# A weight's sign carried through the shift, and a new order of work in steps 0 to 31

## The chip, the cores and the metric

The kernel runs on one core of a Trainium2 chip. A core has a matrix engine (TensorE, PE in the profile, with its weight loads listed apart as PEld), three engines for element-wise work (VectorE or DVE, ScalarE or ACT, GpSimd or POOL) and an engine, SyncE (SP), that here only issues transfers. Each engine works through its own queue in order. Matrices are multiplied from SBUF into PSUM, the memory that sums matmuls; DVE and ACT read and write both, POOL only SBUF. The metric is the device time of one execution in microseconds (us). A difference of about 0.3% is the least that can be told from none.

## The reference

```python
# retention over 8 heads, batch 8, 576 positions, head size 64
scores = scale * np.matmul(q, k.transpose(0, 1, 3, 2))
gamma = 1.0 - 2.0 ** (-5.0 - np.arange(H, dtype=np.float32))
Dmat = np.where(rel >= 0, gamma[:, None, None] ** rel[None, :, :], 0.0)
x = np.matmul(scores * Dmat[None], v)          # then as 4608 x 512
# feed-forward
h = x @ w_in                                   # 512 x 2048, float64
P = a[0] + a[1] * h + a[2] * h**2 + a[3] * h**3
Q = 1.0 + np.abs(b[0]) * np.abs(h) + np.abs(b[1]) * h**2
return ((P / (Q + 1e-06)) @ w_out).astype(np.float32)   # w_out 2048 x 512, float64
```

The two weight matrices are float64 (a float32 array times a float64 scalar), so the kernel gets them as 64-bit words and makes float32 of them itself.

## The kernel before

**Tiling.** The 4608 tokens are 36 units of 128. Retention goes unit by unit, with a running state; a *visit(a, k)* on PE finishes the outputs of unit a and makes scores and state sums of unit k. The feed-forward takes blocks of 512 tokens (four units) and 16 slices f of 128 hidden channels; one (block, slice) is a *step*. Each float32 operand is split in a high and a low part, and a product takes three matmuls, so *gemm1* of a step (x by w_in) is 12 matmuls 128x512 into a PSUM tile `h`, and *gemm2* (the step's result by w_out) 12 more into `acc`, three or four steps later. Between them DVE and ACT make P and Q of 128x512 elements: `ffn_p` (ACT makes p = a3·h + a2 and u = |h|, DVE multiplies p by h), `ffn_p2` (DVE, the last reader of `h`), `ffn_va` and `ffn_v` (ACT, DVE: the denominator), `ffn_r` (ACT: logarithm and exponential, for 1/Q), `ffn_q`, `ffn_q3` (DVE), `ffn_hi` (ACT) and `ffn_lo` (POOL up to step 23, DVE later): the two parts for gemm2. A number in brackets is the step or unit: p2(3) is `ffn_p2` of step 3.

**Two buffers for h.** The pool `ps_h` (line 95) has two tiles. They go in turn to the `h` of each gemm1 and, in a visit with both units, to a tile `y` for unit k. So gemm1 of the step after a visit waits until `ffn_p2` of the step of that visit has read its `h`, and the visit's `y` waits for `ffn_p2` of the step before it.

**Weights.** There are 32 pieces of 128x512 words: (0, f) of w_in, (1, f) of w_out. Each is loaded by SP (line 142) and taken apart by `split_weight` (line 144): ACT writes to a tile `c` the absolute value of the high word, scaled by 2^-112 as if it were a float32 (which turns the exponent field of float64 into that of float32, moved right by three bits), and leaves in place of the low word its top three bits; DVE shifts `c` left by three and puts these in; DVE then puts in the sign; ACT makes the high part of `w`, POOL the low part. These are stages: `start` runs the first, and a call of `splitN` advances each weight that stands at stage N. `split0` does nothing but advance; `split1` is the shift, `split2` the sign, `split3` the last two operations. `STARTS_BEFORE` and `STARTS` (lines 46, 48) set how many weights start when: six before step 0, then 1, 1, 2, 1, 2 and one a step to step 23. So a weight's pace follows from the place of the four `split` names in the list of a step.

**Order.** Nothing is reordered: `InOrder` (line 58) keeps the program's order on each engine, and each step calls the functions in the order of a list of names (`run`, line 513). Before step 0 units 0 to 4 are begun with `BEFORE` and `LAST_BEFORE`. Then steps 0, 2, 4, 6 and 23, which have a visit ("whole" steps), use `FIRST`; steps 1, 3, 5, 7, 21 and 22 `FIRST_ALONE`; steps 8 to 20 `MID` (where u lies in PSUM, in `free_at`); steps 24 to 31 `DENSE` (with a visit) and `DENSE_ALONE`; later ones `REST`, at the end `END`. Steps 0 to 7 are the first half of block 0, steps 8 to 23 block 1, steps 24 to 31 the other half of block 0. All engine instructions pass through one helper and stand on line 67 of the profile; groups are told apart by tile names.

Of the kernel before, what the change touches and what calls it, by code (L numbers as in the profile page):

```python
# [12 lines left out]
F32 = mybir.dt.float32  # L13
# [4 lines left out]
AF = mybir.ActivationFunctionType  # L18
ALU = mybir.AluOpType
# [12 lines left out]

BEFORE = "split1 start scale_q scale_v visit_a decay visit_b add fade keep_hi keep_lo split2 split3 split0".split()
LAST_BEFORE = "visit_b keep_hi visit_a keep_lo start split1 decay add fade scale_q scale_v split2 split3 split0".split()
FIRST = "split1 gemm1 visit ffn_p ffn_p2 ffn_hi split2 decay keep_hi ffn_lo gemm2 ffn_r scale_v scale_q split3 decay1 add fade start split0 keep_lo ffn_q ffn_q3 ffn_va ffn_v".split()
FIRST_ALONE = "split1 split3 gemm1 visit gemm2 ffn_p split2 ffn_va ffn_p2 ffn_hi decay keep_hi ffn_lo ffn_r scale_q decay1 add keep_lo fade start scale_v split0 ffn_q ffn_q3 ffn_v".split()
MID = "start split2 gemm1 ffn_p gemm2 ffn_r ffn_hi ffn_lo ffn_va split3 ffn_p2 ffn_q ffn_v ffn_q3 split0 split1".split()
DENSE = "gemm1 ffn_p visit decay split0 ffn_p2 split1 scale_q ffn_hi ffn_r ffn_va ffn_lo scale_v gemm2 ffn_q split2 ffn_v keep_hi split3 ffn_q3 keep_lo decay1 add fade".split()
DENSE_ALONE = "gemm1 ffn_p visit decay keep_hi decay1 add ffn_r split1 fade keep_lo split2 ffn_p2 split0 ffn_va ffn_v scale_q ffn_hi ffn_lo gemm2 split3 scale_v ffn_q ffn_q3".split()
REST = (  # L40
    "gemm1 ffn_p visit ffn_p2 ffn_hi decay keep_hi ffn_lo decay1 add fade keep_lo scale_q scale_v ffn_va ffn_v gemm2 ffn_r"
    " ffn_q ffn_q3"
# [28 lines left out]
def retention_ffn(ctx: ExitStack, tc: tile.TileContext, qkv, w_in, w_out, ab, masks, gq, gv, out):  # L71
# [26 lines left out]
    pe, act, dve, pool = (InOrder(tc, e) for e in (nc.tensor, nc.scalar, nc.vector, nc.gpsimd))  # L98
# [45 lines left out]
    def split_weight(k):  # L144


        nm = f"{k[0]}_{k[1]}"
        words = bits[k].bitcast(I32).rearrange("p (c w) -> p c w", w=2)
        low, high = words[:, :, 0], words[:, :, 1]
        c = cnv.tile([P, DM], I32, tag="c", name=f"c{nm}")  # L150
        cf = c.bitcast(F32)


        act.activation(cf, high.bitcast(F32), AF.Abs, scale=math.ldexp(1.0, -112))
        act.activation(low, low.bitcast(U32), AF.Copy, scale=math.ldexp(7.49, -32))
        yield
        yield
        dve.scalar_tensor_tensor(c, c, 3, low, ALU.logical_shift_left, ALU.bitwise_or)
        yield
        dve.scalar_tensor_tensor(c, high, -0x80000000, c, ALU.bitwise_and, ALU.bitwise_or)  # L160
        yield
        w = wts.tile([P, 2, DM], F32R, tag=f"w{nm}", name=f"w{nm}")
        del bits[k]
        act.activation(w[:, 0, :], cf, AF.Copy)
        pool.tensor_tensor(w[:, 1, :], cf, w[:, 0, :].bitcast(F32), ALU.subtract)
        parts[k] = w
# [331 lines left out]
    def load_weights(n):  # L498
        for k in [k for _, k in zip(range(n), loads)]:
            load_weight(k)  # L500

    def split_start(n):
        for k in [k for _, k in zip(range(n), splits)]:
            going.append([split_weight(k), 0])
            next(going[-1][0])
# [7 lines left out]
    def run(names, todo):  # L513
        todo |= {f"split{j}": (split_step, j) for j in range(4)}
        for name in names:
            if name in todo:
                todo[name][0](*todo[name][1:])
# [50 lines left out]
    for i in range(len(steps) + lag(len(steps))):  # L568
# [23 lines left out]
        whole = i in VISITS  # L592
        early = FIRST if whole else FIRST_ALONE
        dense = DENSE if whole else DENSE_ALONE
        run(END if not this else MID if free_at else early if i < first else dense if i < 2 * NF else REST, todo)
        load_weights(2)
# [41 lines left out]
```

## Time and profile before

| | |
|---|---|
| median of 3 runs | 917.73 us (916.36 to 919.26) |
| profiled execution, its own time | 915.75 us |
| its span, first to last instruction | 913.9 us |
| mean granted clock of TensorE | 0.983 |
| ACT busy | 696.2 us (76%) |
| POOL busy | 154.3 us (17%) |
| weight pieces split | 32, first ACT operation at 13.2 us, last at 188.2 us |
| gemm1 of step 0 starts | 33.09 us |

A row of a timeline gives the start in us, the duration in us, the engine, the line, the operation, the tiles as written<-read, shapes and count, and in brackets how long the engine had been idle and what released it. A row of windows gives the stretch, its length, and for each engine its busy time with the count of instructions, then the granted clock, the DMA share and GB/s. A row of groups gives the count, then the busy time in us and the mean of one in ns, then idle time before them with its releasers. On PE the rows of matmuls overlap a little, since they are pipelined.

### The profile page before, as it was taken

Reading aid. Unit: us, or ns where it says so; the run is one execution under the profiler, and the core shown is the slowest. Engines: PE = TensorE matmul, PEld = TensorE weight load, DVE = VectorE, ACT = ScalarE, POOL = GpSimd, SP = SyncE. Lnnn points to the kernel's source line nnn. Section 1 sums busy time; section 2 is a strip of 40 time slices with the busy share of each in tenths; the row PEclk is TensorE's granted clock in tenths of the full one; section 3 lists DMA queues with packets and bytes.
Section 4 is the critical chain, followed back from the end, with each engine's and each line's share of the span. In section 5 each row is a group of like instructions: output and inputs, shape, how many; then the busy total and the mean of one; then the engine's idle time right before and its main releaser. Section 6 shows DMA issues by size and latency. Waiting matters only on the chain.

```text
span 913.9 us, 19359 instructions
## 1 busy us (share of the span) xinstructions
PE 888.9 (97%) x7852; PEld 733.1 (80%) x7852; DVE 801.1 (88%) x1217; ACT 696.2 (76%) x1306; POOL 154.3 (17%) x128
## 2 busy tenths in 40 slices
PE   7888999999999999999999999999999999999997
PEld 6666778878888888888888888888888888888886
DVE  3699999998899988889888889889888998888895
ACT  5798899988667778777877787777877777667774
POOL 3556445551011110011100100010110111000000
PEclk8789999999999999999999999999999999999999
DMA  9985000014121112111211112011211121001001
GB/s 340 363 309 202 1 0 1 1 49 138 47 93 48 47 47 93 47 47 47 93 48 48 47 65 74 25 43 33 90 47 48 47 94 47 1 2 46 1 1 46
DMA packets 20569, 65.50 MB, mean 72 GB/s; under 512 B 2432, under 2 KB 2432, under 8 KB 20480
## 3 DMA queue, kind: packets, MB, share of 16 engines
q1 hardware_dynamic: 20480, 64.28, 20.0%
q8 instruction: 61, 1.00, 0.5%
q14 instruction: 28, 0.23, 0.1%
HBM read 54.83 MB, written 9.44 MB: 70 GB/s over the span
## 4 chain that ended last, share of the span: by engine, by line
PE 81%; DVE 13%; issue 2%; ACT 2%; DMA 1%; SPq 0%; ACTq 0%; DVEq 0%
PE acc L67 37%; PE h L67 35%; DVE p L67 6%; PE ps L67 4%; DVE v L67 3%; DVE c L67 3%; PE y L67 2%; PE psNone L67 2%; PE unread L67 1%; DMA gv_sb<-in_gv 1%; ACT free_at L67 1%; DMA bits<-in_w_out 0%; ACT v L67 0%; DVE qk L67 0%; ACT o L67 0%
## 5 line engine op out<-in xcount | busy, mean ns | idle before, releaser
L67 PE MATMUL acc<-w,g 128*128 128x512 f32 x1632 | 396.3, 392 | 0.5 <-DVE o L67 0.3
L67 PE MATMUL h<-xhi,w 128*128 128x512 f32 x1152 | 382.3, 393 | 10.4 <-DVE p L67 6.4
L67 PEld LDWEIGHTS acc<-w,g 128*128 128x128 f32 x1632 | 303.8, 188 | 65.6 <-issue 0.7
L67 PEld LDWEIGHTS h<-xhi,w 128*128 128x128 f32 x1152 | 218.4, 190 | 59.0 <-DVE p L67 8.0
L67 PE MATMUL h<-xlo,w 128*128 128x512 f32 x576 | 226.1, 393 | 0.0
L67 ACT ACTIVATE p<-h,ab_sb 128x512 f32<-128x512 f32 x144 | 111.9, 777 | 127.1 <-PE h L67 117.0
L67 DVE SCALAR_TENSOR_TENSOR p<-p,ab_sb,u 128x512 f32<-128x512 f32 x131 | 120.7, 922 | 15.0 <-ACT u L67 15.0
L67 PEld LDWEIGHTS h<-xlo,w 128*128 128x128 f32 x576 | 109.5, 190 | 22.8
L67 DVE TENSOR_TENSOR p<-p,h 128x512 f32<-128x512 f32 x144 | 98.9, 687 | 29.9 <-ACT u L67 28.9
L67 DVE TENSOR_TENSOR v<-v,u 128x512 f32<-128x512 f32 x131 | 94.7, 723 | 26.5 <-ACT v L67 26.5
L67 ACT ACTIVATE u<-h 128x512 f32<-128x512 f32 x131 | 77.9, 595 | 49.8 <-DVE v L67 49.1
L67 DVE SCALAR_TENSOR_TENSOR p<-p,ab_sb,h 128x512 f32<-128x512 f32 x144 | 107.6, 747 | 4.7
L67 ACT ACTIVATE v<-u,absb 128x512 f32<-128x512 f32 x131 | 105.8, 808 | 1.2 <-DVE p L67 1.1
L67 DVE SCALAR_TENSOR_TENSOR p<-v,p 128x512 f32<-128x512 f32 x144 | 101.3, 703 | 4.4
L67 POOL TENSOR_TENSOR S<-S,gv_sb 128x256 f32<-128x256 f32 x32 | 21.3, 666 | 469.9 <-DVE S L67 446.6
L67 DVE SCALAR_TENSOR_TENSOR v<-v,u 128x512 f32<-128x512 f32 x131 | 95.4, 728 | 0.0
L67 ACT ACTIVATE g<-p 128x512 fp32r<-128x512 f32 x136 | 85.8, 631 | 8.1 <-DVE p L67 3.4
L67 ACT ACTIVATE u<-u 128x512 f32<-128x512 f32 x131 | 83.0, 634 | 4.2
L67 ACT ACTIVATE u<-v 128x512 f32<-128x512 f32 x131 | 81.5, 622 | 0.3 <-DVE v L67 0.3
L67 ACT ACTIVATE kv<-kv,gv_sb 128x64 f32<-128x64 f32 x288 | 72.6, 340 | 8.3 <-DMA gv_sb<-in_gv 5.7
L67 DVE TENSOR_TENSOR g<-p,g 128x512 fp32r<-128x512 f32 x112 | 76.7, 684 | 1.4 <-ACT g L67 1.4
L67 POOL TENSOR_TENSOR qk<-qk,gq_sb 128x512 f32<-128x512 f32 x36 | 56.2, 1562 | 56.7 <-DMA qk<-in_qkv 56.4
(72 smaller groups left out, 715.6 us busy)
## 6 DMA issues: line engine op xcount, KB each, us to landing
qk<-in_qkv SPq DMA_DIRECT2D x36, 512.0 KB, 4.1
kv<-in_qkv SPq DMA_DIRECT2D x36, 512.0 KB, 5.7
bits<-in_w_in SPq DMA_DIRECT2D x16, 512.0 KB, 8.0
bits<-in_w_out SPq DMA_DIRECT2D x16, 512.0 KB, 8.4
out<-o SPq DMA_DIRECT2D x16, 512.0 KB, 4.5
out<-o SPq DMA_DIRECT2D x4, 256.0 KB, 3.6
gq_sb<-in_gq SPq DMA_DIRECT2D x1, 256.0 KB, 2.7
mask_sb<-in_masks SPq DMA_DIRECT2D x1, 32.0 KB, 5.2
```

The costliest lines, as they stand in the source:

```text
L67: return lambda *a, **k: self.tc.keep_in_program_order(method(*a, **k))
```

## The change

The sign operation of DVE is dropped. The ACT operation that scaled the absolute value of the high word becomes a `Prelu`: a word that is positive gets the factor 2^-112 as before, a negative one gets in addition the factor -2^32, which makes it positive and adds 32 to its 8-bit exponent field. That bit, bit 28 of the word, is moved by the shift of three to bit 31, the sign. The stage `split2` stays in the lists as a name but does nothing except advance the weight.

The five lists of steps 0 to 31 get another order. In `FIRST`, `split3` moves in front of `split2` and directly behind `ffn_p`, and `ffn_p2` moves from behind `ffn_p` to behind `decay`, `decay1`, `add`, `start` and `ffn_va`; in `FIRST_ALONE`, `scale_v` and `start` move in front of `ffn_p`, and `ffn_lo`, `ffn_va` behind `ffn_q3`; in `MID`, `split1` moves from the end of a step to the front of the next, and `ffn_r` behind `ffn_hi`.

```diff
-FIRST = "split1 gemm1 visit ffn_p ffn_p2 ffn_hi split2 decay keep_hi ffn_lo gemm2 ffn_r scale_v scale_q split3 decay1 add fade start split0 keep_lo ffn_q ffn_q3 ffn_va ffn_v".split()
-FIRST_ALONE = "split1 split3 gemm1 visit gemm2 ffn_p split2 ffn_va ffn_p2 ffn_hi decay keep_hi ffn_lo ffn_r scale_q decay1 add keep_lo fade start scale_v split0 ffn_q ffn_q3 ffn_v".split()
-MID = "start split2 gemm1 ffn_p gemm2 ffn_r ffn_hi ffn_lo ffn_va split3 ffn_p2 ffn_q ffn_v ffn_q3 split0 split1".split()
-DENSE = "gemm1 ffn_p visit decay split0 ffn_p2 split1 scale_q ffn_hi ffn_r ffn_va ffn_lo scale_v gemm2 ffn_q split2 ffn_v keep_hi split3 ffn_q3 keep_lo decay1 add fade".split()
-DENSE_ALONE = "gemm1 ffn_p visit decay keep_hi decay1 add ffn_r split1 fade keep_lo split2 ffn_p2 split0 ffn_va ffn_v scale_q ffn_hi ffn_lo gemm2 split3 scale_v ffn_q ffn_q3".split()
+FIRST = "split1 gemm1 visit ffn_p split3 scale_q ffn_hi split2 decay scale_v keep_hi ffn_lo gemm2 ffn_r decay1 add fade start ffn_va ffn_p2 keep_lo ffn_q ffn_v ffn_q3 split0".split()
+FIRST_ALONE = "split1 split3 gemm1 visit scale_v start gemm2 ffn_p ffn_p2 ffn_hi split2 decay keep_hi ffn_r scale_q decay1 add keep_lo fade split0 ffn_q ffn_q3 ffn_lo ffn_va ffn_v".split()
+MID = "start split1 gemm1 ffn_p split2 gemm2 ffn_hi ffn_lo ffn_r ffn_va split0 split3 ffn_p2 ffn_q ffn_v ffn_q3".split()
+DENSE = "gemm1 ffn_p visit decay split0 scale_q ffn_p2 split1 ffn_hi ffn_r ffn_va ffn_lo scale_v gemm2 ffn_q split2 ffn_v split3 keep_hi keep_lo decay1 add ffn_q3 fade".split()
+DENSE_ALONE = "gemm1 ffn_p visit decay keep_hi decay1 add ffn_r split1 fade split0 keep_lo split2 ffn_p2 ffn_va ffn_v scale_q ffn_hi ffn_lo gemm2 split3 scale_v ffn_q ffn_q3".split()
...
-        act.activation(cf, high.bitcast(F32), AF.Abs, scale=math.ldexp(1.0, -112))
+        act.activation(cf, high.bitcast(F32), AF.Prelu, scale=math.ldexp(1.0, -112), alpha=-math.ldexp(1.0, 32))
         act.activation(low, low.bitcast(U32), AF.Copy, scale=math.ldexp(7.49, -32))
         yield
         yield
         dve.scalar_tensor_tensor(c, c, 3, low, ALU.logical_shift_left, ALU.bitwise_or)
         yield
-        dve.scalar_tensor_tensor(c, high, -0x80000000, c, ALU.bitwise_and, ALU.bitwise_or)
         yield
```

## The prediction

> **What bounds the kernel now.** I read the head of the page and its slices first, then windows cut where the kind of step changes.
>
> ```profile
> span 913.9 us, 19359 instructions
> ...
> PE 888.9 (97%) x7852; PEld 733.1 (80%) x7852; DVE 801.1 (88%) x1217; ACT 696.2 (76%) x1306; POOL 154.3 (17%) x128
> ...
> PE   7888999999999999999999999999999999999997
> ...
> DMA  9985000014121112111211112011211121001001
> ...
> 33.09:121.36 88.27, 76.02 (x700) 59.93 (x697) 83.59 (x118) 78.29 (x149) 45.56 (x33) 0.92 0.50 180
> 121.36:181.62 60.26, 60.22 (x265) 49.28 (x263) 59.14 (x89) 58.70 (x105) 31.30 (x24) 1.00 0.00 1
> 181.62:260.00 78.38, 77.84 (x945) 64.16 (x944) 70.73 (x113) 61.40 (x130) 19.56 (x17) 1.00 0.25 82
> 260.00:880.00 620.00, 619.59 (x5234) 512.83 (x5233) 553.92 (x846) 460.71 (x842) 46.34 (x41) 1.00 0.15 49
> ```
>
> PE is busy for 97% of the span; what it lacks, it lacks in the first five slices of 22.8 us. The windows say where. From 33.09 (gemm1 of step 0) to 121.36 (gemm1 of step 13) PE is busy 76.02 of 88.27 us, at a clock of 0.92. In steps 13 to 22 it has no idle time (60.22 of 60.26), though DVE and ACT are nearly full too, from 181.62 to 260 it loses 0.54, and then nothing. So what the change does to DVE after 121 can win at most that half microsecond. Before 33 us transfers keep the DMA engines busy (9 in the first two slices), which the change doesn't touch; the three signs there I count at nothing, up to 0.6 won.
>
> What DVE holds up from 33 to 121 I read from the chain of waits in 30:125, and from PE's timeline.
>
> ```profile
> by line: DVE p L67 22.5%; DVE c L67 17.8%; DVE v L67 14.0%; issue 10.6%; DMA bits<-in_w_out 4.3%; ACT free_at L67 4.0%; PE psNone L67 3.3%; ACT v L67 3.2%; PE h L67 3.2%; ACT bits L67 2.5%; ACT c L67 2.4%; ACT o L67 2.0%; DVE xlo L67 1.9%;
> ...
> 41.21 0.50 PE L67 MATMUL h<-xhi,w 128*128 128x512 f32 x1 [2.12 <-DVE p L67]
> ...
> 46.11 0.62 PE L67 MATMUL h<-xhi,w 128*128 128x512 f32 x2
> ...
> 55.16 0.79 PE L67 MATMUL h<-xhi,w 128*128 128x512 f32 x1 [2.66 <-DVE p L67]
> ...
> 60.13 2.92 PE L67 MATMUL acc<-w,g 128*128 128x512 f32 x12
> ...
> 65.70 0.46 PE L67 MATMUL ps<-qk,kv 64*64 64x64 f32 x16
> ...
> 67.89 3.06 PE L67 MATMUL acc<-w,g 128*128 128x512 f32 x12
> ...
> 86.94 0.74 PE L67 MATMUL h<-xhi,w 128*128 128x512 f32 x1 [3.07 <-ACT w L67]
> ...
> 88.43 1.22 PE L67 MATMUL h<-xhi,w 128*128 128x512 f32 x2 [0.32 <-POOL w L67]
> ...
> 91.76 2.89 PE L67 MATMUL acc<-w,g 128*128 128x512 f32 x12
> ...
> 109.84 0.50 PE L67 MATMUL h<-xhi,w 128*128 128x512 f32 x1 [1.59 <-DVE p L67]
> ...
> 118.49 3.03 PE L67 MATMUL acc<-w,g 128*128 128x512 f32 x12 [0.20 <-ACT o L67]
> ...
> 194.08 0.47 PE L67 MATMUL h<-xhi,w 128*128 128x512 f32 x1 [0.54 <-DVE kv L67]
> ...
> 207.26 2.72 PE h L67 x12
> 209.98 2.72 PE acc L67 x12
> ```
>
> The chain is DVE's: p, c and v make 54% of it, and c, the weight tile, alone 17.8%. On PE the last column shows five gaps: 2.12 before step 1, 2.66 before step 3, 3.07 and 0.32 in front of and inside gemm1 of step 7, 1.59 before step 11. The gaps cost more than themselves. A gemm1 or gemm2 takes 2.72 us late in the run, but gemm1(1) lasts from 41.21 to 46.11, 4.9; gemm1(3) from 55.16 to 60.13, 4.97; gemm1(7) from 86.94 to 91.76, 4.82 with its gap of 0.32. That is the low clock behind a gap over 2 us. A visit costs some 2.2 (65.70 to 67.89).
>
> **The change on DVE.** The sign operation:
>
> ```profile
> L67 DVE SCALAR_TENSOR_TENSOR c<-bits,c 128x512 int32<-128x512 int32 x17 | 14.4, 873 | 0.1
> ...
> 39.68 0.69 DVE L67 TENSOR_TENSOR p<-p,h 128x512 f32<-128x512 f32 x1 [0.89 <-ACT u L67]
> 40.41 0.75 DVE L67 SCALAR_TENSOR_TENSOR p<-p,ab_sb,h 128x512 f32<-128x512 f32 x1
> 41.07 1.89 DVE L67 SCALAR_TENSOR_TENSOR c<-bits,c 128x512 int32<-128x512 int32 x3
> 42.88 0.42 DVE L67 TENSOR_TENSOR qk<-y,mask_sb 128x256 f32<-128x256 f32 x1
> ...
> 44.20 0.69 DVE L67 TENSOR_TENSOR xlo<-ps,xhi 128x512 fp32r<-128x512 f32 x1
> ...
> 49.80 0.73 DVE L67 SCALAR_TENSOR_TENSOR p<-p,ab_sb,h 128x512 f32<-128x512 f32 x1
> ...
> 62.97 2.39 DVE L67 SCALAR_TENSOR_TENSOR c<-bits,c 128x512 int32<-128x512 int32 x2
> ...
> 106.01 2.38 DVE L67 SCALAR_TENSOR_TENSOR c<-bits,c 128x512 int32<-128x512 int32 x2
> ...
> 63.11 1.70 POOL L67 TENSOR_TENSOR g<-p,g 128x512 fp32r<-128x512 f32 x1 [3.74 <-DVE p L67]
> ```
>
> 17 of the 32 signs lie in this window, 14.4 us, 873 ns each. Not all of that comes free. The two at 62.97 take 2.39 while POOL works from 63.11 on; an operation with both inputs in SBUF is stretched beside POOL, and with the sign gone the next such operation meets the same POOL work. What a sign costs undisturbed is a pitch of 0.60 (three at 41.07, the next operation at 42.88, 1.81 later), so about 17 x 0.60 = 10.2 us of DVE's 83.59 go. DVE would have some 73 us of work, ACT keeps 78.29: ACT, not DVE, is next to bind.
>
> **The change on ACT.** Prelu stands in place of Abs, with the same tile, shape and an immediate scale:
>
> ```profile
> L67 ACT ACTIVATE c<-bits 128x512 f32<-128x512 f32 x32 | 21.3, 665 | 0.0
> ...
> L99 ACT ACT_TABLE_LOAD x1 | 1.3, 1283 | 0.7 <-PEq L628 0.7
> ...
> 49.87 2.01 ACT L67 ACTIVATE kv<-kv,gv_sb 128x64 f32<-128x64 f32 x8
> ...
> 83.40 0.60 ACT L67 ACTIVATE u<-h 128x512 f32<-128x512 f32 x1 [1.67 <-DVE v L67]
> ...
> 86.27 1.66 ACT L67 ACTIVATE w<-c 128x512 fp32r<-128x512 f32 x3
> ...
> 133.71 0.78 ACT L67 ACTIVATE p<-h,ab_sb 128x512 f32<-128x512 f32 x1
> ...
> 138.97 0.78 ACT L67 ACTIVATE p<-h,ab_sb 128x512 f32<-128x512 f32 x1
> ```
>
> The trace has no Prelu. Below, it could hardly be cheaper than the cheapest of these forms, 0.60 (u<-h at 83.40); above, I take twice 0.665, as if each element went through twice. Abs itself is the nearest row: same input, output and operands. p at 133.71, with two operands from SBUF, takes 0.78; Prelu adds none. So I take 0.665, no change. Steps 13 to 22 have room for little more: ACT takes 138.97 - 133.71 = 5.26 a step against 2 x 2.72 = 5.44 of PE, so Prelu may cost 0.18 more before ACT binds there. The Trainium skill, in "ScalarE activation tables: per-element evaluation and per-set limits", section "What a function is on this engine", says that an ACTIVATE with the same operands costs the same whatever function it evaluates; by that the sum stays as it is. No run here shows it yet.
>
> **The new order, step by step.** I follow PE from step to step.
>
> Step 0: in `FIRST`, p2(0) now stands behind decay, decay1 and add. These four operations take 44.20 - 42.88 = 1.3 us, and they wait for the visit; queued behind them on DVE are p2, keep_lo, q, v, q3, and gemm1(1) waits for p2(0) to give back its `h`. The visit is over at 39 and p2 began at 40.41, so the wait is covered but the four operations are not: gemm1(1) comes at 42.5 rather than 41.21. The three signs at 41.07 stood behind p2 and don't help here. The three weights' `split3`, now ahead of `split2`, goes from step 0 to the head of step 1; its first user is step 3.
>
> Step 1: gemm1(1) ends at 47.4 with the same slow spell. p and u (0.78 and 0.60 on ACT, 1.2 as they overlap), p·h (40.41 - 39.68 = 0.7) and p2 (41.07 - 40.41 = 0.66) follow with no sign between them: p2(1) ends at 50.0, against 50.5 (49.80 + 0.66). scale_v (2.01 at 49.87) and start (two operations of 0.67) now lie in front of p(1), but ACT, freed of the three `w` of step 0, is done with them at 46.5, before gemm1(1) ends. The visit of step 2 needs p2(1).
>
> Step 2: two q, q3, v, shift and p·h, six operations of 0.6 to 0.7, fill DVE until 53.8, then come the four again; p2(2) ends at 55.8, and gemm1(3) starts at 55.95, 0.8 late. So PE's two early gaps get longer, to some 3.4 and 4.
>
> Step 3: p2(3) stood behind two signs (62.97, 2.39) and began after 65.3. Now p, u, p·h and p2 follow gemm1(3), which ends at 60.9: p2(3) ends at 63.6. From here PE sets the pace: gemm2(0) to 63.6, gemm1(4) to 66.4, visit to 68.6, gemm2(1) to 71.4. p2(4), again behind the four operations, ends at 70.3, so gemm1(5) needn't wait: it starts at 71.4, gemm2(2) at 74.1, gemm1(6) at 76.8, the outputs of the last early unit at 79.5 (no new unit, 1.5 by estimate from a visit's 2.2), gemm2(3) at 81.0, to 83.8.
>
> Step 7: gemm1(7) waited for `w` of piece (0,7), whose high part is one of the three at 86.27. It stood behind u(6) (83.40), which waited 1.67 for v on DVE, and behind hi, keep_hi and `ffn_r`. In the new `FIRST` `split3` follows `ffn_p` directly: p(6) at 79.6, u to 80.8, `w` to 81.4, POOL's part, at the 1.70 of the like operation at 63.11, to 83.1. PE is free at 83.8 and doesn't wait, so its low clock goes too: gemm1(7) ends at 86.5 rather than 91.76, **5.2 us ahead**.
>
> Steps 8 to 12: the gap of 1.59 at 109.84 was behind p2, and that behind two signs of 2.38 at 106.01; with them gone p2 is 2 us earlier and the gap closes. So does the 0.20 at 118.49. That is 5.2 + 1.6 + 0.2 = **7.0**.
>
> Steps 13 to 31: PE has no gaps to give except 0.54 at 194.08, behind a DVE that had signs before it: **0.5**. `MID` and `DENSE` only shift work under full PE; the 0.7 that DVE gains a step is idle time. `visit` keeps its place, and with it SP's loads; POOL has 45.56 of 88.27 us of work, and no order moves its load past what PE needs.
>
> The margins at gemm1(5) and gemm1(7) are 1.1 and 0.7 us, and one operation stretched beside POOL (2.39 for two rather than 1.2) can use up one of them: I take off 0.8. **Sum: 7.0 + 0.5 - 0.8 = 6.7 us** on the profiled execution's 915.75 (span 913.9), 909.05. The median of the runs is 1.98 above that execution, so 911.0.
>
> **Rivals.**
> *ACT takes over early.* In 33 to 121 ACT has idle time of 9.98 us, spread in waits that a new order may keep. It is busy for 88.7% of this window and 97.4% of the next (58.70 of 60.26). If the change takes it a third of that way, to 91.6%, the window lasts 78.29 / 0.916 = 85.5: 2.8 won, 914.9. For it: ACT's fixed order, the longer early gaps. Against: by the steps above no wait of PE on ACT is left from step 4 on.
> *More comes in.* At 97.4% the window takes 80.4, 7.9 won; with 0.5 at 194 and 0.6, one sign before step 0 that PE may have waited for, 9.0: 908.7.
> *The order gives it back.* If p2 behind decay keeps PE waiting in all four whole steps, 4 x 1.3 = 5.2 and a slow spell of 1.8 after gemm1(5), 7.0 in all, eat the gain: 917.5. It decides once DVE reaches p2(4) over 1.1 us later than I have it.
> *Prelu is slow.* At 1.33, 11 weights at 121 to 181 lose 11 x (0.665 - 0.18) = 5.3, and 17 before them 17 x 0.665 = 11.3 if ACT binds there: 16.6 - 6.7 = 9.9 slower, 927.6. From 1.08 each (11 x 0.24 + 17 x 0.42 = 9.8) it is slower than before by over 0.3%. Against it: Abs, Identity, Copy, Ln and Exp of this shape all lie near 0.6 to 0.8 here.
> *A table is loaded for Prelu.* The trace has one ACT_TABLE_LOAD, 1283 ns, for Abs, Copy, Identity, Ln and Exp. If Prelu weren't among its functions, ACT would load twice a weight, 64 x 1.283 = 82 us: about 990. The Trainium skill, same page and section, says just that: functions of different sets are one such load of 1283 ns apart, and the trace agrees on that figure.
>
> **How the numbers follow.** Forecast 0.50, ACT early 0.20 (0.12 of it just past 0.3%), more 0.10, given back 0.12 (0.03 of it slower), Prelu slow 0.06, table 0.02. 0.3% of 917.73 is 2.75 us, about what a measurement can tell from no change, so faster means below 915.0: 0.50 + 0.12 + 0.10 = 0.72. Slower 0.03 + 0.06 + 0.02 = 0.11, same 0.17. From 907.0 to 916.0 lie the forecast, the case of more and the early ACT, 0.80.
>
> **What would show it.** Right: no c<-bits,c on DVE; Prelu at 0.66 to 0.68; the first gaps a little longer; no gap before steps 7 and 11; gemm1(13) near 115; one table load. Wrong: a PE gap before step 5 or 7, ACT w waiting for DVE, or gaps in steps 13 to 31.

## The result and the profile after

The changed kernel takes **904.3 us** (median of 4 runs, 903.88 to 908.05) against 917.43 for the kernel before (4 runs, 916.36 to 919.26): a ratio of 0.9864, 95% interval 0.9833 to 0.9895. The forecast was 911.0 with a range of 907.0 to 916.0; the direction came true, and the time lies below the range. The profiled execution took 904.02 us, 11.73 less than the 915.75 of the one before; the forecast had 6.7.

First the head and the slices of the page of the changed kernel, as they were shown for the kernel before.

```profile
span 902.2 us, 19318 instructions
...
PE 882.2 (98%) x7852; PEld 729.1 (81%) x7852; DVE 779.8 (86%) x1185; ACT 693.9 (77%) x1306; POOL 154.5 (17%) x128
...
PE   7889999999999999999999999999999999999997
...
PEclk9799999999999999999999999999999999999999
...
PE 89%; ACT 6%; DVE 3%; DMA 1%; issue 1%; POOL 0%; SPq 0%; ACTq 0%; POOLq 0%
```

DVE has 32 instructions fewer (1217 to 1185) and is busy 21.3 us less (801.1 to 779.8). PE's slices reach 9 from the fourth on, one slice earlier. The last line is the share of each engine in the chain that ended last: PE makes 89% of it.

Then windows of the changed kernel (stretch, length, busy time and count for PE, PEld, DVE, ACT, POOL, then clock, DMA share, GB/s).

```profile
33.09:121.36 88.27, 82.06 (x742) 66.10 (x742) 79.79 (x114) 86.18 (x165) 50.09 (x37) 0.97 0.49 178
33.09:62.00 28.91, 23.83 (x356) 19.18 (x359) 25.56 (x37) 28.51 (x66) 17.73 (x14) 0.92 0.95 350
62.00:90.00 28.00, 27.38 (x268) 21.72 (x259) 27.59 (x40) 26.67 (x47) 16.36 (x12) 1.00 0.54 198
90.00:121.36 31.36, 30.84 (x136) 25.20 (x135) 26.64 (x39) 31.00 (x54) 16.00 (x12) 1.00 0.00 1
```

In the same 88.27 us PE is busy 82.06 (76.02 before), ACT 86.18 (78.29), DVE 79.79 (83.59). The three parts show what the long window hides: to 62 us ACT is full (28.51 of 28.91), from 62 to 90 DVE (27.59 of 28.00), then ACT again (31.00 of 31.36), and from 62 on PE lacks about 1.1 us in all.

The waits of PE in that window (what it waited for, us in total, times, longest), and the rows of its timeline that answer to those of before:

```profile
PE h L67 <- DVE kv L67: 5.5, 3, 3.0
PE acc L67 <- ACT o L67: 0.5, 1, 0.5
```

```profile
40.35 0.47 PE L67 MATMUL h<-xhi,w 128*128 128x512 f32 x1 [2.10 <-DVE kv L67]
...
44.54 0.62 PE L67 MATMUL h<-xhi,w 128*128 128x512 f32 x2
...
52.96 0.47 PE L67 MATMUL h<-xhi,w 128*128 128x512 f32 x1 [2.98 <-DVE kv L67]
...
55.80 2.88 PE L67 MATMUL acc<-w,g 128*128 128x512 f32 x12
...
67.10 0.47 PE L67 MATMUL h<-xhi,w 128*128 128x512 f32 x1 [0.41 <-DVE kv L67]
...
82.66 3.14 PE L67 MATMUL acc<-w,g 128*128 128x512 f32 x12
```

The gaps before steps 7 and 11 (3.07, 0.32, 1.59) are gone; those before steps 1 and 3 remain (2.12 to 2.10, 2.66 to 2.98), now released by `kv`, the early sum of `decay`, and not by `p`. New are 0.41 before step 5 and 0.52 before gemm2(8), behind ACT's `o`. gemm2(0), at 60.13 before, starts at 55.80; gemm2(4), at 91.76 before, at 82.66.

Last the groups of the changed operation (count, busy us, mean ns) and of the table load:

```profile
L67 ACT ACTIVATE c<-bits 128x512 f32<-128x512 f32 x32 | 21.2, 662 | 0.0
L99 ACT ACT_TABLE_LOAD x1 | 1.3, 1283 | 0.7 <-PEq L627 0.7
```

Prelu costs 662 ns, Abs cost 665, and there is still one table load.

### The profile page after: what moved, and what is told of

It reads as the page before. It is cut to its first block, busy times and chain, and to the rows that moved or that the text cites. A ratio compares the mean times of both kernels' runs of the same rounds, so it can differ in the third digit from the quotient of the medians.

```text
span 902.2 us, 19318 instructions
## 1 busy us (share of the span) xinstructions
PE 882.2 (98%) x7852; PEld 729.1 (81%) x7852; DVE 779.8 (86%) x1185; ACT 693.9 (77%) x1306; POOL 154.5 (17%) x128
## 4 chain that ended last, share of the span: by engine, by line
PE 89%; ACT 6%; DVE 3%; DMA 1%; issue 1%; POOL 0%; SPq 0%; ACTq 0%; POOLq 0%
PE acc L67 42%; PE h L67 39%; PE ps L67 4%; PE y L67 2%; PE psNone L67 1%; DVE p L67 1%; ACT u L67 1%; DVE v L67 1%; ACT bits L67 1%; ACT w L67 1%; DMA bits<-in_w_out 1%; ACT c L67 1%; ACT kv L67 1%; ACT p L67 1%; DMA qk<-in_qkv 0%
## 5 line engine op out<-in xcount | busy, mean ns | idle before, releaser
L67 DVE SCALAR_TENSOR_TENSOR p<-p,ab_sb,u 128x512 f32<-128x512 f32 x131 | 117.9, 900 | 15.7 <-ACT u L67 15.6
L67 DVE TENSOR_TENSOR v<-v,u 128x512 f32<-128x512 f32 x131 | 97.0, 741 | 25.5 <-ACT v L67 25.5
L67 DVE SCALAR_TENSOR_TENSOR p<-v,p 128x512 f32<-128x512 f32 x144 | 104.2, 724 | 4.3
L67 DVE SCALAR_TENSOR_TENSOR v<-v,u 128x512 f32<-128x512 f32 x131 | 93.2, 711 | 0.0
```

Source lines behind the costliest of these rows:

```text
L67: return lambda *a, **k: self.tc.keep_in_program_order(method(*a, **k))
```

## The experiments

The medians of the kernel before were 917.4 to 917.7 in the runs below, so medians can be compared across them.

**The two halves of the change, each alone.** The first kernel is the one before with the Prelu and without the sign; the second is the changed one with Abs and the sign in `split2`.

```diff
-        act.activation(cf, high.bitcast(F32), AF.Abs, scale=math.ldexp(1.0, -112))
+        act.activation(cf, high.bitcast(F32), AF.Prelu, scale=math.ldexp(1.0, -112), alpha=-math.ldexp(1.0, 32))
...
-        dve.scalar_tensor_tensor(c, high, -0x80000000, c, ALU.bitwise_and, ALU.bitwise_or)
```

> The Prelu without sign operations, in the old order. If DVE's time was what the change was worth (theory A), most of the 13 us are here: 905 to 908, with the gaps of PE before steps 3 and 7 gone. If the order makes the larger part (theory B), DVE gets lighter by some 10 us but w of piece (0,7) still stands behind hi, keep_hi and ffn_r, so a gap of 1 to 3 us stays before step 7: 911 to 914. If neither works without the other, within 2 us of 917.

> The new order with Abs and the sign operations kept (the sign in split2, which now stands behind split3, so the weight is still whole when it is used). Theory A: DVE stays full from step 1 on and the order wins little: 915 to 919. Theory B: split3 directly behind ffn_p closes the gap before step 7 by itself: 908 to 912. In both, the sign stands in front of decay in the whole steps and gemm1 of the next step comes later by 0.6 per sign than in the changed kernel.

Prelu alone: 909.07 us, ratio 0.9911 (0.9896 to 0.9927). The order alone: 920.11, 1.0027 (1.0018 to 1.0036). So Prelu wins 8.4, the order by itself loses 2.6, and beside Prelu it wins 4.8 (909.07 to 904.3). Neither time lies in a range that was expected. PE's timeline of Prelu alone shows what the old order left:

```profile
53.43 0.50 PE L67 MATMUL h<-xhi,w 128*128 128x512 f32 x1 [2.08 <-DVE p L67]
...
82.69 0.50 PE L67 MATMUL h<-xhi,w 128*128 128x512 f32 x1 [1.56 <-ACT w L67]
...
84.05 0.73 PE L67 MATMUL h<-xhi,w 128*128 128x512 f32 x2 [0.63 <-POOL w L67]
...
87.98 2.98 PE L67 MATMUL acc<-w,g 128*128 128x512 f32 x12
```

The step 7 wait is still there, as theory B had it, with a gemm1 of 5.29 us (82.69 to 87.98) behind it; most of the 13 us is won all the same, as theory A had it. DVE's timeline of the order alone shows why it loses:

```profile
40.51 1.89 DVE L67 SCALAR_TENSOR_TENSOR c<-bits,c 128x512 int32<-128x512 int32 x3
42.31 0.42 DVE L67 TENSOR_TENSOR qk<-y,mask_sb 128x256 f32<-128x256 f32 x1
42.65 0.41 DVE L67 TENSOR_TENSOR kv<-S,y 128x256 f32<-128x256 f32 x1
```

With signs in it, `split2` of the new `FIRST` puts them in front of `decay` and the early sum, and PE's first gaps become 3.89 and 4.11, both behind `kv`; the first is 1.79 longer than in the changed kernel, three signs at 0.6. The wait for `w` in step 7 shrinks to 0.54 even so, and gemm2(4) comes 1.85 earlier than in the kernel before (89.91), but gemm2(0) 2.7 later (62.84) and gemm2(8) 1.2 later (119.72). The order is made for a `split2` that does nothing.

**The places of single names.** Each kernel is the changed one with one thing moved back: p2 directly behind `ffn_p` in `FIRST`; `split3` behind `ffn_r` in `FIRST`; the old `MID`, `DENSE` and `DENSE_ALONE`; `scale_v` and `start` behind `ffn_p2` in `FIRST_ALONE`; and `start` alone there.

```diff
-FIRST = "split1 gemm1 visit ffn_p split3 scale_q ffn_hi split2 decay ... start ffn_va ffn_p2 keep_lo ffn_q ffn_v ffn_q3 split0".split()
+FIRST = "split1 gemm1 visit ffn_p ffn_p2 split3 scale_q ffn_hi split2 decay ... start ffn_va keep_lo ffn_q ffn_v ffn_q3 split0".split()
...
+FIRST = "split1 gemm1 visit ffn_p scale_q ffn_hi split2 decay scale_v keep_hi ffn_lo gemm2 ffn_r split3 decay1 add ...".split()
...
-FIRST_ALONE = "split1 split3 gemm1 visit scale_v start gemm2 ffn_p ffn_p2 ffn_hi split2 ...".split()
+FIRST_ALONE = "split1 split3 gemm1 visit gemm2 ffn_p ffn_p2 scale_v start ffn_hi split2 ...".split()
...
+FIRST_ALONE = "split1 split3 gemm1 visit scale_v gemm2 ffn_p ffn_p2 start ffn_hi split2 ...".split()
```

> The changed kernel with ffn_p2 of the whole steps back behind ffn_p, in front of decay. By the step of the prediction (gemm1 of the next step waits for p2 behind four operations) this gives back 1.3 us at steps 1 and 3: some 2.6 us faster than the changed kernel, 901 to 902. By the new theory (the next gemm1 takes the tile of y, given back by decay and the early sum, since these now come ahead of p2) the wait changes its owner but not its end: gemm1 of step 1 starts within 0.3 us of 40.35, and the time is within 1.5 us of the changed kernel, 903 to 906.

> The changed kernel with split3 of the whole steps back behind ffn_r. If its place is what closes the gap before step 7, w of piece (0,7) comes some 2.2 us later on ACT (behind hi, keep_hi and the two of ffn_r), PE stands 1 to 2 us before step 7, perhaps with a spell of low clock: 906 to 908. If DVE alone closed it, no gap and 904.

> The changed kernel with MID, DENSE and DENSE_ALONE (steps 8 to 20 and 24 to 31) as before. Theory: PE is full there with either order, so the time stays within 1 us of the changed kernel: 903.5 to 905.5. Rival: the new MID and DENSE carry part of the 4.8 us that the order wins beside Prelu: 906 to 909.

> The changed kernel with scale_v and start of the steps without a visit behind ffn_p and ffn_p2 again. If ACT holds up p of steps 1 and 3 (45.60 against a gemm1 that ends at 44.54; 59.44 against 55.80), p2 of these steps comes 1 to 3.5 us earlier and PE stands less before the visit and step 3: 902 to 903.5. If the later start and scale_v come due later instead (weights of step 5 and 6, unit 7), no gain or a loss: 904 to 907.

> The changed kernel with only the start order of FIRST_ALONE moved back behind ffn_p2; scale_v stays ahead of p. In the changed kernel scale_v (42.56) and start (44.47) stand ahead of p(1) (45.60), whose gemm was over at 44.54. Theory (ACT is the bound from 33 to 121 us, and any work that fills its wait for PE is a gain): p(1) comes about 1 us earlier, but start then has to be done behind p, so nothing is gained: 903 to 905, same. Rival (a gelu that comes late is what costs): p(1) at about 44.6 and p(3) at about 58.3 instead of 59.44, and some 1 us less at the end: about 902.7 to 903.3.

| moved back | median us | ratio (95%) |
|---|---|---|
| p2 of `FIRST` | 903.97 | 0.9853 (0.9837 to 0.9868) |
| `split3` of `FIRST` | 908.04 | 0.9889 (0.9872 to 0.9905) |
| `MID`, `DENSE`, `DENSE_ALONE` | 904.39 | 0.9858 (0.9845 to 0.9872) |
| `scale_v` and `start` | 907.56 | 0.9895 (0.9881 to 0.9908) |
| `start` alone | 905.22 | 0.9864 (0.9851 to 0.9877) |

p2's move and the three later lists are worth nothing that these runs can show. `split3` is worth 3.7 by the medians and 2.4 by the profiled executions (906.37 against 904.02): PE's timeline of that kernel has the step 7 wait back.

```profile
81.46 0.50 PE L67 MATMUL h<-xhi,w 128*128 128x512 f32 x1 [1.42 <-ACT w L67]
...
82.82 0.73 PE L67 MATMUL h<-xhi,w 128*128 128x512 f32 x2 [0.63 <-POOL w L67]
```

`scale_v` and `start` are worth 3.3 together, `start` alone at most the 0.9 between two medians whose ranges overlap; of the 1.26 between the two profiled executions 0.86 were there at gemm1(1) (41.21 against 40.35), ahead of any name that moved. The prices of single names don't add up to the 4.8, and `ffn_lo` and `ffn_va` of `FIRST_ALONE` were not moved back alone. ACT's timeline, first of the kernel with both moved back, then of the changed one, shows the trade (kv<-kv,gv_sb is `scale_v`; u<-v and u<-u are `ffn_r`):

```profile
43.88 0.78 ACT L67 ACTIVATE p<-h,ab_sb 128x512 f32<-128x512 f32 x1 [2.31 <-PE h L67]
44.56 0.59 ACT L67 ACTIVATE u<-h 128x512 f32<-128x512 f32 x1
45.03 2.01 ACT L67 ACTIVATE kv<-kv,gv_sb 128x64 f32<-128x64 f32 x8
...
48.74 0.63 ACT L67 ACTIVATE u<-u 128x512 f32<-128x512 f32 x1
```

```profile
42.56 2.03 ACT L67 ACTIVATE kv<-kv,gv_sb 128x64 f32<-128x64 f32 x8
...
45.60 0.78 ACT L67 ACTIVATE p<-h,ab_sb 128x512 f32<-128x512 f32 x1
...
47.41 0.63 ACT L67 ACTIVATE u<-u 128x512 f32<-128x512 f32 x1
```

Moved back, ACT waits 2.31 us for gemm1(1) and then does `scale_v` in front of `ffn_r`; DVE waits for that (2.75, at 49.40), and the gap before gemm1(3) grows from 2.98 to 5.50. In the changed order that wait of ACT is filled, p(1) comes a little late, and nothing is lost by that: without `start` ahead of it p(1) came 4.62 behind the start of gemm1(1) rather than 5.25, yet gemm1(3) came 12.90 behind it rather than 12.61. So the rival by which a late p costs (two of the expectations call p and what follows it a gelu) fell.

**The clock.** To see what the half clock behind a gap costs, matmuls 128x128 that nobody reads fill PE's gaps after the visits of steps 0 and 2, in the changed kernel and in the one before.

```diff
+            if k in FILL:
+                t = ps_acc.tile([P, 2, 512], F32, tag="acc", name=f"fill{k}")
+                for _ in range(FILL[k]):
+                    pe.matmul(t[:, 0, 0:P], gq_sb[:, 0], gq_sb[:, 0], start=True, stop=True)
```

> The changed kernel with 6 and 9 matmuls of 128x128, whose result nobody reads, in PE's gaps behind the visits of steps 0 and 2, so that the granted clock does not fall in gemm1 of steps 1 and 3. If the clock in these steps sets the end, 1.5 us or more are won: 902 to 903, and runs like the one of 908 go. If ACT hides it (p of step 1 starts at 45.60 behind start, though gemm1 of step 1 is over at 44.54), the clock is at 1.00 and the time the same, 903.5 to 905.

> The kernel before with 6 and 8 such matmuls in the same gaps. If DVE set the pace of steps 1 to 5 there, the low clock of gemm1(1) and gemm1(3), 2.2 us each, was hidden and the time stays at 916.5 to 918. If the low clock was part of the loss, 2 to 4 us are won: 913.5 to 915.5, and as much of the change's 13 us came from a spell that no longer counts.

In the changed kernel nothing comes of it: 903.99, ratio 0.9859 (0.9845 to 0.9872), though the last matmul of gemm1(1) began 2.6 us behind the first rather than 4.2 (40.35 to 44.54). p(1) still starts at 45.57, behind ACT's queue. In the kernel before it wins 1.4: 915.97, 0.9986 (0.9977 to 0.9995), between the two forecasts. Most of the low clock was hidden there as well: in the profiled executions gemm2(0) came 2.4 earlier (57.72 against 60.13), gemm1(7) only 0.84 (86.10 against 86.94), and 0.80 of that was there at gemm1(1).

**Which engine binds the changed kernel.** ACT's 97.6% from 33 to 121 (86.18 of 88.27) made me think that ACT alone does, with DVE having 8.5 us to spare. So the copies of the high part of `w` went to DVE, for 13 weights and for 6 of them, the latter also with `start` moved back.

```diff
-        act.activation(w[:, 0, :], cf, AF.Copy)
+        if 3 <= order.index(k) < 16:
+            dve.tensor_copy(w[:, 0, :], cf)
+        else:
+            act.activation(w[:, 0, :], cf, AF.Copy)
```

> The changed kernel with the copies of the high part of the weights 3 to 15, in the order made, done by DVE instead of ACT: some 0.52 us each off ACT, 13 of them, 6.8 us; DVE gets them at some 0.35 to 0.7 us each, 4.5 to 9 us. Theory (ACT, 86.18 of 88.27 us busy from 33 to 121, is the bound of the changed kernel, and DVE with 79.79 has 8.48 to spare): faster by 2 to 5 us, 899 to 902, with no wait for ACT's w left on PE; if the copies take 0.7 us, DVE is the bound again and the time is 903 to 907. Rival (PE's own matmuls bound the stage by now, 82.06 of 88.27): 903 to 905, same, with the PE gaps where they are.

> As the run with all the copies by DVE, but only the weights 5, 7, 9, 11, 13 and 15: 3.1 us off ACT, 2 to 4 us on DVE, so that neither has more than its stretch. Theory (ACT is the bound): faster by 1.5 to 3 us, 901 to 902.5. Rival (PE is the bound by now): 903 to 905, same.

> The kernel with six copies by DVE and start behind ffn_p2, together. Theory (ACT is the bound): the copies alone count, 901 to 902.5. Rival (the late gelus of steps 1 and 3 cost): 1 us less than with the copies alone.

All were slower than the changed kernel: 910.71, ratio 0.9922 (0.9907 to 0.9936); 908.92, 0.9903 (0.9890 to 0.9917); 907.62, 0.9891 (0.9877 to 0.9905). The last two can't be told apart. So this theory fell. The windows of the kernel with 13 copies on DVE show where, and a row of its PE shows how:

```profile
33.09:121.36 88.27, 78.97 (x715) 63.02 (x715) 79.57 (x119) 74.64 (x142) 44.32 (x35) 0.94 0.49 180
...
62.00:90.00 28.00, 26.00 (x281) 20.21 (x280) 27.73 (x40) 20.59 (x35) 14.61 (x11) 0.94 0.58 203
```

```profile
83.20 0.50 PE L67 MATMUL h<-xhi,w 128*128 128x512 f32 x1 [1.06 <-DVE w L67]
```

ACT lost 11.5 us in the long window and PE did 3.1 less. From 62 to 90 DVE is as full as before (27.73 of 28.00): the copies stand in its queue behind its other work, `w` comes late, and the wait of step 7 is back (1.06 for DVE, then 0.74 for POOL's part), with a clock of 0.94 in that stretch. From gemm1(5) to gemm1(8) this kernel falls from 2.2 to 5.8 us behind the changed one (69.34 and 91.42 against 67.10 and 85.63). With six copies the wait for POOL's `w` in step 7 is 0.65 and 0.61. The spare time of DVE was real, but in the changed kernel only 0.41 of the 8.48 us lie from 62 to 90; 3.35 lie before and 4.72 behind.

The theory that replaced it: the engines bind in turn, ACT to 62 us, DVE to 87, ACT again, and PE is close behind (from 62 us on, that is: before, it lacks 5.08 of 28.91). The chain of waits of the changed kernel from 33 to 125 (start, length, what) says the same:

```profile
41.00 1.67 ACT w L67 x3
42.67 1.91 ACT kv L67 x8
45.72 0.66 ACT p L67
...
65.01 0.69 DVE c L67
65.70 0.60 DVE p L67
...
71.47 1.78 DVE p L67
...
93.25 1.04 ACT w L67 x2
...
107.07 0.95 ACT o L67
108.07 3.03 PE acc L67 x12
```

Three kernels then leave work out: ACT's operation on the low words for ten weights (the shift then joins the raw low words by an `and`, not shown in the diff), DVE's shift for thirteen weights, and both.

```diff
+        rounds = not 6 <= order.index(k) < 16
+        if rounds:
-        act.activation(low, low.bitcast(U32), AF.Copy, scale=math.ldexp(7.49, -32))
+            act.activation(low, low.bitcast(U32), AF.Copy, scale=math.ldexp(7.49, -32))
...
+        if not 3 <= order.index(k) < 16:
-        dve.scalar_tensor_tensor(c, c, 3, low, ALU.logical_shift_left, ALU.bitwise_or)
+            dve.scalar_tensor_tensor(c, c, 3, low, ALU.logical_shift_left, ALU.bitwise_or)
```

> The changed kernel without ACT's operation on the low words of the weights 6 to 15 in the order made (so their low words are not rounded, and DVE's shift puts them in by an and in place of an or): ten operations of a pitch of 0.56 us less on ACT, those now at 39.75, 45.04, 53.50, 54.62 and 58.89 and five from 68 to 84. Theory (the engines bind in turn: ACT to 62 us, DVE to 87, ACT again, with PE close behind everywhere): two of them stand ahead of p(1) and come off the wait before gemm1(3), at most 1.1; the others give little: 902 to 903.5. Rival (ACT binds all the way): 5.6 less, about 898.7. Rival (DVE binds by itself): 904, same.

> The changed kernel without DVE's shift of the weights 3 to 15 in the order made (so these weights are left unshifted): 13 operations of 0.6 to 1.8 us less on DVE, those now from 33.96 to 95.63. Theory (the engines bind in turn, PE close behind): 0.6 comes off the wait before gemm1(3) (the shift at 50.88), and of the 5 us that DVE gains from 62 to 87 only PE's gaps there and behind, 0.41 and 0.52, can be won: 1 to 1.6, 902.4 to 903.3. Rival (DVE binds all the way): 8 us less, about 896. Rival (ACT binds by itself): 904, same.

> The changed kernel without either: no operation of ACT on the low words of the weights 6 to 15, no shift of DVE for the weights 3 to 15. Theory (PE is close behind): 1.1 before gemm1(3) for ACT, 0.6 for DVE, 0.9 for the gaps behind: 901.5 to 902.5, less than 3 us better than the changed kernel though some 14 us of work are gone. Rival (ACT and DVE cover each other, and PE has more to give): 5 us or more.

903.73, ratio 0.9850 (0.9837 to 0.9864); 903.11, 0.9844 (0.9830 to 0.9857); 902.60, 0.9835 (0.9821 to 0.9850). They win 0.6, 1.2 and 1.7 us, where a bound by ACT or DVE all the way asked for 5.6 or 8. From gemm1(1) to gemm1(3) the three take 11.68, 11.98 and 10.89 us against 12.61: 0.9, 0.6 and 1.7 less, where 1.1, 0.6 and 1.7 were expected. The windows of the third:

```profile
62.00:90.00 28.00, 27.88 (x300) 23.03 (x300) 24.07 (x33) 24.63 (x43) 14.35 (x11) 1.00 0.55 199
90.00:121.36 31.36, 31.36 (x140) 25.93 (x139) 25.90 (x39) 31.00 (x53) 16.34 (x13) 1.00 0.00 1
```

From 62 us on PE is busy for 59.24 of 59.36 us: it is the bound there once a little is taken off ACT and DVE. In the changed kernel it lacked 1.14 of the same 59.36. Before 62 us that kernel's PE still lacks 5.71 of 28.91 with ACT busy for 27.71; what a much lighter ACT would win there, no run tests. The intervals of these three and of the changed kernel overlap, so it is the order of size that they settle, and the windows that show why. No kernel tried is faster than the changed one by more than these intervals.

## Why the prediction went wrong, step by step

The profiled executions differ by 11.7 us, the forecast for them was 6.7. PE's rows split the difference (each entry is how much further ahead PE came in that stretch):

| stretch | forecast | measured |
|---|---|---|
| to the start of gemm2(0) (60.13 to 55.80) | -0.8 | 4.33 |
| from there to gemm2(4), past step 7 (91.76 to 82.66) | 6.0 | 4.77 |
| from there to gemm2(8) (118.49 to 108.07) | 1.8 | 1.32 |
| behind | 0.5 | 1.31 |
| margin taken off | -0.8 | |
| sum | 6.7 | 11.73 |

**The failed step is the wait of gemm1(1) and gemm1(3) in steps 0 to 3.** The forecast had gemm2(0) at 60.9; it came at 55.80, 5.1 earlier, as much as the whole error. The larger half, 2.6, is one wrong step made twice: gemm1 of the next step was said to wait for p2 behind "these four operations", which were to make its gap longer by 1.3. It stayed at 2.10. DVE's timeline of the changed kernel:

```profile
39.46 0.42 DVE L67 TENSOR_TENSOR qk<-y,mask_sb 128x256 f32<-128x256 f32 x1
39.80 0.41 DVE L67 TENSOR_TENSOR kv<-S,y 128x256 f32<-128x256 f32 x1
...
40.79 0.74 DVE L67 SCALAR_TENSOR_TENSOR p<-p,ab_sb,h 128x512 f32<-128x512 f32 x1
```

gemm1(1) starts at 40.35, when the second of them is over and before p2(0) has begun: it takes the tile of `y`, which the early sum gives back, and not that of h(0). With p2 put first the releaser is `p` again (gaps of 2.12 and 2.92) and the time the same, 903.97, since p2 takes as long as those two operations (0.66). So "waits until p2 has read h" was a property of the old order, not of the two buffers: in these kernels the tile that comes free first is taken. The 5.1 are these parts.

*1.3, the wait of gemm1(1).* Both kernels start gemm1(1) 9.16 behind ACT's copy `xhi` of the last early unit, so nothing of the order delays it:

```profile
32.05 0.60 ACT L67 ACTIVATE xhi<-psNone 128x512 fp32r<-128x512 f32 x1 [2.02 <-PE psNone L67]
```

```profile
31.19 0.60 ACT L67 ACTIVATE xhi<-psNone 128x512 fp32r<-128x512 f32 x1 [3.67 <-PE psNone L67]
```

*0.86, ahead of step 0.* The second row, of the changed kernel, is that much earlier than the first, of the one before. But in kernels with the same program up to there the copy began at 30.08 (`scale_v` and `start` back) and at 32.05 (`start` back), and at 31.23 in the kernel before with its gaps filled. Executions differ by that much, so the 0.86 is not shown to be the change.

*0.84, from gemm1(1) to gemm1(3).* They start 12.61 us apart rather than the 13.45 forecast (42.5 to 55.95; 13.95 in the kernel before). The same wrong step gives 1.27: from the start of the operation behind p2(1) to gemm1(3) it took 4.68 (48.28 to 52.96, released by `kv`), where the forecast had 5.95 from p2(1)'s end. The way from gemm1(1) to p2(1)'s end took 0.43 more, 7.93 rather than 7.5. There the forecast erred twice. It gave gemm1(1) 4.9, but took the row at 46.11 for its end, which belongs to gemm1(2) (ACT's p(1) starts at 45.53, before that). Counted by its 12 matmuls, gemm1(1) took 4.08 before (41.21 to 45.29) and 4.42 after (40.35 to 44.77). And ACT was to be done with `scale_v` and `start` before gemm1(1) ends; p(1) started at 45.60, 0.83 behind that end. Among "five gaps" on PE the prediction also left out two in visits, 0.87 behind POOL's `qk` at 37.70 and this one of step 2, which waits for p2(1) (over at 50.5):

```profile
50.64 0.27 PE L67 MATMUL y<-qk 64*64 64x64 f32 x2 [1.21 <-issue]
```

It is gone in the changed kernel. With Prelu alone, in the old order, gemm1(1) and gemm1(3) are 12.14 apart, so what was won here against the kernel before is the signs', and the order gives 0.47 back.

*2.11, the clock in gemm1(3).* It was given 4.95 as before, and took 2.84 in this execution, without a half clock behind its gap. In the kernel with p2 put first it took 4.04 (52.83 to 56.87), the half clock was back, and the time was the same: gemm1(4) came 1.52 later than in the changed kernel (60.04 against 58.52), gemm2(8) 0.14 earlier (107.93). The waits at 67.10 and 108.07, 0.41 and 0.52 in the changed kernel and none and 0.28 in that one, make up 0.65 of it, the rest lies in small parts. So this part is no lasting gain by itself, as the filled gaps also showed; like the 0.86 it is what these executions happened to draw.

**Steps 4 to 7: the mechanism was right.** `split3` behind `ffn_p` removes the wait for `w`, shown by the kernel that puts it back. That one has its gaps of 1.42 and 0.63 at a clock of 1.00 in the profiled execution; the low clock stands behind the like gaps of Prelu alone (0.58 from 84.05 to 87.98). 4.8 of 6.0 came: 0.41 is the wait left at 67.10, the rest lies in small parts over the matmuls and visits of these steps. A gap before step 5 was one of the prediction's signs of being wrong, and its margin of 1.1 there did not hold: PE was free there at 66.7 rather than the 71.4 forecast, just ahead of the early sum.

**Steps 8 to 12:** the gap behind p2 closed as forecast; a new one of 0.52 behind ACT's `o` took part of it. **Steps 13 to 31:** the gap at 194.08 is gone, and the three lists add nothing, both as forecast. That gap cost 0.94 and not 0.54 (PE is 10.76 ahead from step 15 on, 11.70 from gemm1(26)), and another 0.34 was won about gemm1(14), which started 2.92 behind gemm2(9) before and 2.72 after. gemm1(13), by the prediction's signs near 115, came at 110.94. **The margin** of 0.8 for stretched operations was not needed: DVE's operations ahead of the wait at 67.10 took no longer than usual (0.68 to 0.75).

**DVE and ACT.** That DVE was the bound held: taking the signs off alone wins 8.4. That ACT is next held in two of three stretches, and that PE "sets the pace" from step 4 holds to within 1.1 us. Of the rivals, "more comes in" was the nearest: it asked for ACT at 97.4% of the window and got 97.6%, but its 908.7 was still too high. "The order gives it back" (its 7.0 on top of the forecast's 911.0 make 918.0, not 917.5) did not come: p2(4) started at 67.54, where the forecast had its end at 70.3. The order does lose without the Prelu (920.11), but by signs in front of `decay`, not by p2. The slow Prelu and the second table load are excluded by 662 ns and one load. The Trainium skill's rule that the prediction cites ("ScalarE activation tables: per-element evaluation and per-set limits", "What a function is on this engine") is borne out by the 662 beside 665.

**The median.** The forecast added 1.98, the distance of the old median from the old profile. The changed kernel's median lies 0.28 above its profile. This 1.7 and the 5.0 above are the 6.7 between 911.0 and 904.3; why one profiled execution lay below its median and the other near it is not shown, but the copy of the last early unit shows that executions differ by up to 2 us before step 0.

## What to carry to other kernels

Cut a window where its limit changes before reading spare time from it: DVE's 8.5 us to spare over 88 us were 0.4 in the 28 us in which late work of DVE held PE up. When an operation moves behind others, ask which of the buffers its waiter can take comes free first, rather than carry over the owner seen in the old trace. And an engine's wait for another is the place for its deferrable work: `scale_v` there was worth more than a p that starts a microsecond earlier.

## What the runs showed of the hardware

*A gap of 2 us already brought a half clock, and one of 3 us not always.* In the changed kernel the window from 40 to 44 us, behind a gap of 2.10, has a granted clock of 0.62, and 54 to 58, behind one of 2.98, has 1.00; with p2 put first the second, behind 2.92, has 0.57. Behind 2.12 in the kernel with Prelu alone gemm1(1) ran at 1.00 (2.87 us).

```profile
40.00:44.00 4.00, 3.65 (x10) 2.90 (x11) 4.00 (x7) 4.00 (x12) 2.90 (x3) 0.62 0.94 312
...
54.00:58.00 4.00, 4.00 (x19) 3.32 (x18) 3.98 (x6) 4.00 (x12) 1.93 (x3) 1.00 1.00 391
```

```profile
54.00:58.00 4.00, 4.00 (x13) 3.10 (x12) 4.00 (x6) 4.00 (x13) 2.17 (x3) 0.57 1.02 395
```

In both traces the half clock of these windows is a spell of 3.41 us at 0.50, from 41.00 to 44.41 and from 54.37 to 57.78. The Trainium skill, "TensorE: Matmul & The Clock Gate", section "What's actually happening", describes a free-running window of some 3.4 us. That the same gap falls differently from one execution to the next fits this; that 2.1 us were enough is not what its row on the idle state says.

*A copy that is cheaper on another engine can still lose.* In the kernel with 13 copies on DVE most single copies of `w` took 0.41 us there, with a mean of 0.58; on ACT a single one of the changed kernel takes 0.62 (at 50.22). That kernel took 6.4 us longer, with the copies late in DVE's full stretch and PE waiting for them in step 7.
